# A new instruction order for a fused recurrence and mixture-of-attention kernel, with three small jobs allowed on ScalarE

## The chip, the cores and the metric

The kernel runs on one core of a Trainium2 chip. The metric is the device time of one launch in microseconds (us), lower is better; the median of three runs counts. The core has five engines that run side by side and wait for each other by semaphores: TensorE (PE; its weight loads are listed as PEld), VectorE (DVE), ScalarE (ACT), GpSimd (POOL) and SyncE (SP), which here only issues DMA transfers.

## The reference

The first half is a recurrence over 768 steps for 4 batches and 8 heads with a 48x48 state; its output, rearranged, is the input of the second half, a mixture of four causal attention experts of which each token uses two.

```python
def _attn_ref(r, k, v, w, u):
    for t in range(S):
        kt, vt, rt, wt = (k[:, :, t], v[:, :, t], r[:, :, t], w[:, :, t])
        cur = np.einsum('bhd,bhe->bhde', u[None] * kt, vt)
        y[:, :, t] = np.einsum('bhd,bhde->bhe', rt, state + cur)
        state = wt[:, :, :, None] * state + np.einsum('bhd,bhe->bhde', kt, vt)
    return y

def _moe_ref(x, w_gate, wq, wk, wv, wo):
    logits = x @ w_gate                       # the top K = 2 of E = 4 experts get softmax weights w
    for e in range(E):
        q = x @ wq[e]; k = x @ wk[e]; v = x @ wv[e]
        scores = scale * (q @ k.transpose(0, 2, 1))
        scores = np.where(causal, -1000000000.0, scores)
        a = np.exp(scores - scores.max(-1, keepdims=True))
        a /= a.sum(-1, keepdims=True) + 1e-09
        ye = a @ v @ wo[e]
        for kk in range(K):
            mask = topk[:, :, kk] == e
            out += mask[..., None] * w[:, :, kk:kk + 1] * ye
```

## The kernel before

**Tiling.** The work is cut into eight units (b, g): four batches, and the two halves of 384 steps of each. A unit's recurrence runs over four pairs of heads (p = 0 to 3) in chunks of 64 steps. For each pair SyncE loads the decays, keys and queries (`lt`), the values and keys in natural order (`nat`) and the values (`vy`). VectorE and GpSimd form running products of the decays (`w`, `suf`, lines 518 to 524), scaled keys and queries (`kt` L531, `pre` L533) and the bonus of the current step (`rk`; in the first unit `nat<-lt` L501, in the others `uk` L538, which needs the loaded `u_sb`, and `ur` L542). TensorE transposes the keys (`ktp`), makes the state updates (`ups` L403) and the products inside a chunk (`aps` L587). VectorE masks these (`am` L592) and carries the state from chunk to chunk (`wst` L414, five or six short instructions in a row for each pair). The states are scaled once more (`ys` L424), and TensorE sums up the output (`yps`, L356 and L358). The attention half then runs projections (`pp` L684, `vp` L722), scores (`sp` L789), the row maximum on VectorE (L800), the exponential on ScalarE (L805), transposes (`tp`), weighted sums (`yp` L847), gates and the output projection (`op` L915).

**What sets the order.** Each of these jobs is entered with `plan.add`, with the engines that it may run on. No scheduler decides anything at run time: the table `ORDER` lists every job as a letter for its engine (P, V, A, G, S for TensorE, VectorE, ScalarE, GpSimd, SyncE) and its number. The instructions are issued in exactly this order, so each engine has a fixed queue in which nothing overtakes. Which buffer a tile gets also follows from the table.

Three rules lie on top of the table. A transfer on SyncE waits for the last TensorE instruction that stands ahead of it in the table (`reason="pace"`); a transfer that stands ahead of every product waits for none. GpSimd's two-input jobs wait for the last such job of VectorE ahead of them (`reason="port"`). And a transpose is written as whole products or as two halves, by the mode that TensorE is in when the job comes (`way`).

TensorE works in several tilings: whole array for projections, quarters for the recurrence, halves of rows or columns for scores, half transposes and weighted sums. The table decides how often neighbours in TensorE's queue differ in tiling.

The table also places 14 "warming" products (`warm`, L967), 128x512 products of constants whose results nobody reads. They only keep TensorE busy while the first loads come in.

## Time and profile before

| | |
|---|---|
| time, median of 3 runs | 324.02 us (323.98 to 326.83) |
| profiled execution, its own time | 323.66 us |
| its span, first to last instruction | 321.9 us |
| busy share of the span: PE, PEld | 95%, 77% |
| busy share: DVE, ACT, POOL | 85%, 73%, 46% |
| chain that ended last: PE, DVE, DMA | 75%, 12%, 4% |

The span is 1.76 us shorter than the profiled execution's time; the rest lies around it. The busy time of PE is that of pipelined products whose ends are modelled, so that a PE shown as busy may still have been held up a little. The profile gives busy times by stretch, what ended each idle time of an engine (in square brackets in the rows below), and the chain of work followed back from the last instruction.

### The profile page before, as it was taken

Reading aid. Unit: us, or ns where it says so; the run is one execution under the profiler, and the core shown is the slowest. Engines: PE = TensorE matmul, PEld = TensorE weight load, DVE = VectorE, ACT = ScalarE, POOL = GpSimd, SP = SyncE. Lnnn points to the kernel's source line nnn. Section 1 sums busy time; section 2 is a strip of 40 time slices with the busy share of each in tenths; the row PEclk is TensorE's granted clock in tenths of the full one; section 3 lists DMA queues with packets and bytes.
Section 4 is the critical chain, followed back from the end, with each engine's and each line's share of the span. In section 5 each row is a group of like instructions: output and inputs, shape, how many; then the busy total and the mean of one; then the engine's idle time right before and its main releaser. Section 6 shows DMA issues by size and latency. Waiting matters only on the chain.

```text
span 321.9 us, 13382 instructions
## 1 busy us (share of the span) xinstructions
PE 304.9 (95%) x5334; PEld 247.6 (77%) x5338; DVE 273.0 (85%) x870; ACT 236.4 (73%) x852; POOL 148.3 (46%) x284
## 2 busy tenths in 40 slices
PE   4878999999999899999999999999999999999995
PEld 2755667778876786899887878799888976978684
DVE  6988999999999999999999998977877736575762
ACT  2359799798999898897699776566757664567962
POOL 2225436567375756844667847675121010320420
PEclk9999999999999999999999999999999999999999
DMA  7999574762672789447266472502000001000022
GB/s 230 336 273 227 159 199 142 189 170 60 150 243 75 188 220 227 146 99 195 90 152 178 103 208 72 165 22 88 2 27 0 27 26 52 19 32 24 2 75 74
DMA packets 17758, 39.98 MB, mean 124 GB/s; under 512 B 2592, under 2 KB 10528, under 8 KB 17696
## 3 DMA queue, kind: packets, MB, share of 16 engines
q1 hardware_dynamic: 17696, 39.13, 43.0%
q8 instruction: 42, 0.69, 1.0%
q14 instruction: 20, 0.16, 0.2%
HBM read 34.40 MB, written 4.72 MB: 122 GB/s over the span
## 4 chain that ended last, share of the span: by engine, by line
PE 75%; DVE 12%; DMA 4%; issue 3%; ACT 2%; POOL 2%; SPq 1%; DVEq 0%; ACTq 0%; POOLq 0%
PE pp L684 12%; PE sp L789 11%; PE yp L847 11%; PE op L915 8%; PE vp L722 7%; PE tp L232 5%; PE aps L587 4%; PE ups L403 3%; PE tp L228 2%; PE yps L356 2%; PE yps L358 2%; DMA nat<-in_nat_dram 2%; PE pp L677 2%; DMA lt<-in_wkr_dram 2%; PE ktp L232 2%
## 5 line engine op out<-in xcount | busy, mean ns | idle before, releaser
L805 ACT ACTIVATE a<-a,mx 128x128 f32<-128x128 f32 (+5 forms) x96 | 64.2, 671 | 8.8 <-DVE mx L800 8.6
L800 DVE CUSTOM_DVE_ANT_0 a<-sp,causal 128x128 f32<-128x128 f32 (+5 forms) x96 | 56.6, 614 | 11.0 <-PE sp L789 9.0
L236 ACT COPY ATa<-tp 128x512 f32<-128x512 f32 (+3 forms) x75 | 36.3, 499 | 9.6 <-PE tp L232 8.0
L847 PE MATMUL yp<-ATa,v_sb 128*64 128x384 f32 (+2 forms) x240 | 35.8, 430 | 0.0
L414 DVE SCALAR_TENSOR_TENSOR wst<-wst,suf,ups 112x48 f32<-112x48 f32 x160 | 33.3, 253 | 1.8 <-ACT wst L236 1.3
L684 PE MATMUL pp<-xh,wh_qk 128*128 128x384 f32 x84 | 31.8, 379 | 0.9 <-issue 0.9
L559 ACT ACTIVATE xn<-nat,rk 128x48 f32<-128x48 f32 x126 | 30.7, 329 | 1.0 <-DVE rk L552 1.0
L789 PE MATMUL sp<-K,Q 64*128 64x384 f32 (+4 forms) x160 | 31.1, 420 | 0.4
L684 PE MATMUL pp<-xh,wl_qk 128*128 128x384 f32 x84 | 28.4, 338 | 0.0
L684 PE MATMUL pp<-xl,wh_qk 128*128 128x384 f32 x84 | 28.2, 336 | 0.0
L232 PEld LDWEIGHTS tp<-ident,a 64*128 64x128 f32 x520 | 21.4, 138 | 6.1 <-issue 1.9
L358 PE MATMUL yps<-ys,pre 64*64 64x48 f32 (+1 forms) x704 | 24.7, 220 | 1.1 <-issue 0.6
L232 PE MATMUL tp<-ident,a 64*128 64x64 f32 x520 | 25.3, 226 | 0.4 <-DVE lg L728 0.4
L904 POOL TENSOR_TENSOR yl<-yr,yh 128x384 fp32r<-128x384 f32 x12 | 12.0, 1007 | 29.2 <-ACT yh L903 22.6
L356 PE MATMUL yps<-vy,am 64*64 64x48 f32 x768 | 25.2, 219 | 0.0
L847 PEld LDWEIGHTS yp<-ATa,v_sb 128*64 128x64 f32 x240 | 15.3, 136 | 12.8 <-issue 9.5
L424 POOL TENSOR_TENSOR ys<-wst,suf 112x240 f32<-112x240 f32 (+1 forms) x29 | 23.2, 809 | 3.3 <-DVE wst L414 2.4
L358 PEld LDWEIGHTS yps<-ys,pre 64*64 64x64 f32 (+1 forms) x704 | 21.8, 133 | 3.2 <-POOL ys L424 1.4
L356 PEld LDWEIGHTS yps<-vy,am 64*64 64x64 f32 x768 | 22.6, 134 | 0.1
L550 ACT ACTIVATE nat<-nat 128x48 f32<-128x48 f32 x96 | 22.0, 243 | 0.0
L789 PEld LDWEIGHTS sp<-K,Q 64*128 64x128 f32 x160 | 15.3, 186 | 8.1 <-issue 3.7
L592 DVE TENSOR_TENSOR am<-aps,dec_mask 64x384 f32<-64x384 f32 (+1 forms) x35 | 19.1, 552 | 1.4 <-ACT am L598 0.7
(161 smaller groups left out, 914.3 us busy)
## 6 DMA issues: line engine op xcount, KB each, us to landing
lt<-in_wkr_dram SPq DMA_DIRECT2D x56, 218.6 KB, 3.9
nat<-in_nat_dram SPq DMA_DIRECT2D x28, 432.0 KB, 4.2
vy<-in_vY_dram SPq DMA_DIRECT2D x32, 144.0 KB, 3.5
out_dram<-ob SPq DMA_DIRECT2D x24, 192.0 KB, 1.9
lt<-in_wkr_dram SPq DMA_DIRECT2D x3, 583.0 KB, 5.6
w_qk<-in_wqk_dram SPq DMA_DIRECT2D x1, 768.0 KB, 7.3
nat<-in_nat_dram SPq DMA_DIRECT2D x4, 144.0 KB, 6.7
w_vg<-in_wvg_dram SPq DMA_DIRECT2D x1, 390.0 KB, 7.1
```

Source lines behind the costliest of these rows:

```text
L232: nc.tensor.transpose(o()[:, h * 512 + i * 64:h * 512 + i * 64 + 64], src[r], ident[r, r])
L236: nc.scalar.copy(o, i)
L356: nc.tensor.matmul(to, am()[k, c, :], vy()[k, c, :], start=zero and x == 0, stop=not first and i == 2 and x == len(group) - 1)
L358: nc.tensor.matmul(to, pre()[r, c, 0:C], ys()[r, c, :], start=i == x == 0, stop=False)
L414: nc.vector.scalar_tensor_tensor(new, ws[0:112, c0 + c - 1, :], sfv()[0:112, c, 0:1], upk()[0:112, o], op0=ALU.mult, op1=ALU.add)
L559: nc.scalar.mul(xn()[:, i, (2 * p + h) * D:(2 * p + h + 1) * D], v()[:, i, h, :], rk()[:, i, h:h + 1])
L684: nc.tensor.matmul(pp()[:, 0:384], w[:, qk, k, cs], x()[:, k, :], start=(k == j == 0), stop=(k == j == 2))
L789: nc.tensor.matmul(spv(x)[:, h, :], q_()[p, t], flat(k_())[p, o], start=j == 0, stop=j == len(terms) - 1)
L800: nc.vector.tensor_tensor_reduce(out=a()[:, 0:n].rearrange("p (a n) -> p a n", a=np_), in0=spv(x), in1=causal[:, S - n:S].rearrange("p (a ...
L805: plan.add("exp", {"ACT": t_exp(n)}, lambda e, x=x, y=y, mx=mx, a=a: nc.scalar.activation(a()[:, 0:n], a()[:, 0:n], AF.Exp, bias=mx(), sca ...
L847: nc.tensor.matmul(yp()[e * 64:e * 64 + 64, lo:hi], v_sb[ep]()[:, j, e * 64:e * 64 + 64], at, start=(j == 0), stop=(j == nj - 1))
L915: nc.tensor.matmul(op()[:, 0:DM], y()[:, t], w[:, ep, :], start=(j + ep == 0), stop=(j == 2 and ep == 1))
```

## The change

Three kinds of job get ScalarE as a further choice: scaling the states (`ys`, there as one multiplication for each chunk), the eviction of the gate logits (`lg`, 128x4), and the eviction of the transposed gate weights (`gT`). And the table `ORDER` is replaced as a whole; it still holds the same work and 14 warming products.

```diff
                 def scaled(e, ys=ys, ws=ws, sfv=sfv):
                     o = slice(1 - g, NH)
+                    if e == "ACT":
+                        for c in range(1 - g, NH):
+                            nc.scalar.mul(ys()[0:112, c, :], ws[0:112, c0 + c - 1, :], sfv()[0:112, c, 0:1])
+                        return
...
-                plan.add("ys", {"DVE": t_dve((NH - 1 + g) * D), "POOL": 680 if g == 0 else 645}, scaled, [suf] + [kw + (c0 - g + c,) for c in range(NH - 1 + g)], [ys])
+                plan.add("ys", {"DVE": t_dve((NH - 1 + g) * D), "POOL": 680 if g == 0 else 645, "ACT": 227 * (NH - 1 + g)}, scaled, [suf] + [kw + (c0 - g + c,) for c in range(NH - 1 + g)], [ys])
...
-            plan.add("lg", {"DVE": 70}, lambda e: nc.vector.tensor_copy(lg()[:, i, :], vp()[:, 256:260]), [vp], [(lg, i)])
+            plan.add("lg", {"DVE": 70, "ACT": 100}, lambda e: copy(e, lg()[:, i, :], vp()[:, 256:260]), [vp], [(lg, i)])
...
-            plan.add("gT", {"DVE": 131}, lambda e: nc.vector.tensor_copy(gT(), gp()[0:GROWS, 0:128]), [gp], [gT])
+            plan.add("gT", {"DVE": 131, "ACT": 168}, lambda e: copy(e, gT(), gp()[0:GROWS, 0:128]), [gp], [gT])
...
 ORDER = """
-S110 S111 V1 V2 V117 P13 P21 V118 S3 S137 V114 S136 V119 S170 V122 P33 S195 V121 S113 V120 V123 V142 V139 V124
+S110 V1 V2 V117 S111 V118 V119 S3 S136 S112 S113 S195 S170 P26 P23 P10 V120 V114 V121 S137 V122 V123 V142 V139
...
```

Counted over the whole program, by the tables: `lg` stands 18 times of 24 on ScalarE, `gT` 5 times of 9, `ys` 5 times of 32 (27 multiplications). Of the jobs that had a choice already, many have another engine now. VectorE gives up 4 `uk` and 4 `ur` (GpSimd has them), 2 `pre`, 3 of the value evictions, 2 half-height masks, 1 `kts`, 1 `ys` and 11 short evictions of transposes (128 or 256 columns). It takes on 4 `kt`, 5 evictions of queries and keys, 5 longer evictions of transposes (384 or 512 columns), 2 `ob`, 2 `yl`, 2 `rk`, 2 `rw` (L529) and one each of `w`, `xn` (L561), `wst` copy and full-height mask. That is 51 instructions off VectorE and 26 on. GpSimd's jobs are 6 fewer. On TensorE the places where neighbours differ in tiling are 171 instead of 174; one transpose job is written in halves instead of whole.

The first place is SyncE's queue in the first 20 us. Names: `lt0` to `lt3` are the four buffers of a pair's streams (the second load of `lt0` and `lt1` is for the second unit), `nat000` is unit (0, 0), pair 0, `nat010` unit (0, 1), pair 0. Before, rows 9 to 18 of the queue:

```order
L245 DMA nat000_129<-in_nat_dram 128x288
L245 DMA vy002_150<-in_vY_dram 128x288
L442 DMA lt0_66<-in_wkr_dram 48x1166 x2
L245 DMA vy001_160<-in_vY_dram 128x288
L245 DMA w_qk_169<-in_wqk_dram 128x1536
L442 DMA lt1_67<-in_wkr_dram 48x1166 x2
L245 DMA w_vg_228<-in_wvg_dram 128x780
L245 DMA nat002_167<-in_nat_dram 128x288
L245 DMA nat010_268<-in_nat_dram 128x864
L962 DMA u_sb_90<-in_uN_dram 128x384
```

Of the change, rows 3 to 13 of the queue:

```order
L965 DMA u_t_91<-in_uT_dram 128x8
L245 DMA lt1_67<-in_wkr0_dram 128x1166
L245 DMA nat000_125<-in_nat_dram 128x288
L245 DMA vy000_127<-in_vY_dram 128x288
L245 DMA lt2_68<-in_wkr0_dram 128x1166
L245 DMA lt3_69<-in_wkr0_dram 128x1166
L245 DMA nat001_140<-in_nat_dram 128x288
L446 DMA lt0_66<-in_wkr_dram 48x1166 x2
L966 DMA u_sb_90<-in_uN_dram 128x384
L245 DMA vy001_201<-in_vY_dram 128x288
L245 DMA w_qk_219<-in_wqk_dram 128x1536
```

`nat000` moved from row 9 to row 5, `lt1` one row forward (it stood behind `nat001` in row 4), and `u_sb` from row 18 to row 11, ahead of `w_qk`; `w_vg` went back from row 15 to row 24. Farther on, `lt2` and `lt3` are loaded for the second unit in both; the load that VectorE takes first of the two is now the first one issued.

The second place is VectorE's queue at the second and third pair of the first unit. Names: `w2001` is the decay product of unit (0, 0), pair 1, and `nat001` its bonus. Before, rows 17 to 28:

```order
L518 TENSOR_TENSOR w2001_144<-lt1_67 128x199
L501 TENSOR_TENSOR nat001_127<-lt1_67 128x2x192
L533 TENSOR_TENSOR pre000_147<-lt0_66,w2000_118 128x2x192
L520 SCALAR_TENSOR_TENSOR suf001_152<-w2001_144,one_suf_72 128x198
L527 TENSOR_TENSOR lt1_67<-lt1_67 128x192
L522 RECIPROCAL inv_pre_75<-suf001_152 128x6
L518 TENSOR_TENSOR w2002_158<-lt2_68 128x199
L529 TENSOR_TENSOR lt1_67<-lt1_67 128x192
L531 TENSOR_TENSOR kt001_163<-lt1_67,suf001_152 128x2x192
L520 SCALAR_TENSOR_TENSOR suf002_165<-w2002_158,one_suf_72 128x198
L501 TENSOR_TENSOR nat002_167<-lt2_68 128x2x192
L524 SCALAR_TENSOR_TENSOR w2001_144<-w2001_144,inv_pre_75 128x198
```

Of the change, rows 17 to 28:

```order
L522 TENSOR_TENSOR w2001_145<-lt1_67 128x199
L505 TENSOR_TENSOR nat001_140<-lt1_67 128x2x192
L524 SCALAR_TENSOR_TENSOR suf001_148<-w2001_145,one_suf_72 128x198
L537 TENSOR_TENSOR pre000_150<-lt0_66,w2000_117 128x2x192
L526 RECIPROCAL inv_pre_75<-suf001_148 128x6
L533 TENSOR_TENSOR lt1_67<-lt1_67 128x192
L528 SCALAR_TENSOR_TENSOR w2001_145<-w2001_145,inv_pre_75 128x198
L531 TENSOR_TENSOR lt1_67<-lt1_67 128x192
L522 TENSOR_TENSOR w2003_157<-lt2_68 128x199
L505 TENSOR_TENSOR nat003_159<-lt2_68 128x2x192
L535 TENSOR_TENSOR kt001_184<-lt1_67,suf001_148 128x2x192
L537 TENSOR_TENSOR pre001_238<-lt1_67,w2001_145 128x2x192
```

Pair 3 now comes ahead of pair 2 (its streams are in `lt2`), and the same number of rows stands ahead of the first job on `lt1`.

The third place is TensorE's queue at the start. Before, rows 1 to 12:

```order
L967 LDWEIGHTS causal
L967 MATMUL warm_120<-causal 128x512
L967 LDWEIGHTS causal
L967 MATMUL warm_122<-causal 128x512
L967 LDWEIGHTS causal
L967 MATMUL warm_135<-causal 128x512
L509 MATMUL rk_180<-u_t,nat_129 64x1 x12
L232 MATMUL ktp_197<-ident,kt_142 128x64 x6
L509 MATMUL rk_206<-u_t,nat_127 64x1 x12
L967 LDWEIGHTS causal
L967 MATMUL warm_222<-causal 128x512
L228 MATMUL ktp_224<-ident,kt_163 128x128 x3
```

Of the change, rows 11 to 20 (five warming products stand ahead of these rows):

```order
L971 LDWEIGHTS causal
L971 MATMUL warm_165<-causal 128x512
L971 LDWEIGHTS causal
L971 MATMUL warm_167<-causal 128x512
L971 LDWEIGHTS causal
L971 MATMUL warm_169<-causal 128x512
L513 MATMUL rk_171<-u_t,nat_125 64x1 x12
L232 MATMUL ktp_186<-ident,kt_143 128x64 x6
L513 MATMUL rk_203<-u_t,nat_140 64x1 x12
L403 MATMUL ups_221<-nat_125,kts_196 64x48
```

Eight warming products now stand ahead of the first real one instead of three, and the last of the 14 stands right behind the first `aps`; before, five stood behind the first `yps`, and one came far later. The first `ups`, which needs `nat000`, comes ahead of the second `ktp` instead of behind it.

## Rows read from the trace of the kernel before

**Rows 1.** The page: the span, then busy us, share and instructions by engine.
```profile
span 321.9 us, 13382 instructions
...
PE 304.9 (95%) x5334; PEld 247.6 (77%) x5338; DVE 273.0 (85%) x870; ACT 236.4 (73%) x852; POOL 148.3 (46%) x284
```
**Rows 2.** By stretch: length, busy us of each engine, granted clock, DMA share, GB/s.
```profile
16.00:60.00 44.00, 38.81 (x943) 28.15 (x942) 41.02 (x123) 36.16 (x166) 20.77 (x33) 1.00 0.73 197
60.00:190.00 130.00, 127.93 (x2462) 105.78 (x2461) 125.83 (x401) 112.48 (x433) 83.39 (x143) 1.00 0.59 157
190.00:310.00 120.00, 119.73 (x1709) 98.74 (x1703) 88.54 (x290) 79.62 (x231) 40.28 (x96) 1.00 0.13 43
...
16.00:40.00 24.00, 19.92 (x521) 14.14 (x519) 21.21 (x64) 18.30 (x78) 9.64 (x16) 1.00 0.82 219
```
**Rows 3.** The page: the chain that ended last, shares by engine.
```profile
PE 75%; DVE 12%; DMA 4%; issue 3%; ACT 2%; POOL 2%; SPq 1%; DVEq 0%; ACTq 0%; POOLq 0%
```
**Rows 4.** Timeline of VectorE, 0 to 42 us: start, us, instruction, [idle before, releaser].
```profile
7.35 0.37 DVE L518 TENSOR_TENSOR w<-lt 128x199 f32<-128x199 f32 x1 [0.47 <-DMA lt<-in_wkr_dram]
...
16.25 1.02 DVE L592 TENSOR_TENSOR am<-aps,dec_mask 128x384 f32<-128x384 f32 x2 [0.21 <-PE aps L587]
...
22.83 0.46 DVE L538 TENSOR_TENSOR nat<-nat,u_sb 128x288 f32<-128x288 f32 x1 [0.94 <-DMA u_sb<-in_uN_dram]
...
28.61 0.37 DVE L518 TENSOR_TENSOR w<-lt 128x199 f32<-128x199 f32 x1 [0.75 <-DMA lt<-in_wkr_dram]
```
**Rows 5.** Timeline of SyncE's queue, 0 to 45 us: the issues behind those waits.
```profile
2.85 0.43 SPq L245 DMA_DIRECT2D nat<-in_nat_dram  x1
3.33 1.38 SPq L245 DMA_DIRECT2D lt<-in_wkr_dram  x3
...
16.25 0.33 SPq L962 DMA_DIRECT2D u_sb<-in_uN_dram  x1
...
21.04 2.59 SPq L442 DMA_DIRECT2D lt<-in_wkr_dram  x4
```
**Rows 6.** Waits of SyncE's queue, 0 to 60 us: us in total, times, longest.
```profile
SPq L962 <- PE aps L587: 1.6, 1, 1.6
```
**Rows 7.** Groups by form: busy us, mean ns, idle before.
```profile
L414 DVE SCALAR_TENSOR_TENSOR wst<-wst,suf,ups 112x48 f32<-112x48 f32 x160 | 33.3, 253 | 1.8 <-ACT wst L236 1.3 <-PE ups L403 0.3
...
L538 DVE TENSOR_TENSOR nat<-nat,u_sb 128x288 f32<-128x288 f32 x20 | 10.2, 508 | 0.9 <-DMA u_sb<-in_uN_dram 0.9
...
L531 DVE TENSOR_TENSOR kt<-lt,suf 128x384 f32<-128x384 f32 x13 | 7.4, 582 | 0.0
...
L728 DVE COPY lg<-vp 128x4 f32<-128x4 f32 x24 | 3.7, 153 | 1.9 <-ACT v_sb L236 1.4 <-PE vp L722 0.4
...
L882 DVE COPY gT<-gp 128x128 bf16<-128x128 bf16 x9 | 1.9, 213 | 0.7 <-PE gp L881 0.7
...
L236 ACT COPY wst<-ups 112x48 f32<-112x48 f32 x13 | 2.4, 203 | 4.8 <-DVE wst L414 2.9 <-PE ups L403 1.9
```
**Rows 8.** Timeline, 14 us: runs of short instructions on VectorE and ScalarE.
```profile
14.09 1.47 ACT L559 ACTIVATE xn<-vy,rk 128x48 f32<-128x48 f32 x6
14.14 1.49 DVE L414 SCALAR_TENSOR_TENSOR wst<-wst,suf,ups 112x48 f32<-112x48 f32 x8
```
**Rows 9.** Timeline of TensorE's weight loads around 218 us.
```profile
218.26 0.19 PEld L722 LDWEIGHTS vp<-wl_vg,xh 128*128 128x128 f32 x1
218.38 0.19 PEld L722 LDWEIGHTS vp<-wh_vg,xl 128*128 128x128 f32 x1
218.71 0.79 PEld L587 LDWEIGHTS aps<-pre,kt 64*64 64x64 f32 x48
```
**Rows 10.** Groups by form, PEld: first 0 to 16 us, then 16 to 60 us.
```profile
L587 PEld LDWEIGHTS aps<-pre,kt 64*64 64x64 f32 x48 | 2.7, 205 | 0.0
...
L587 PEld LDWEIGHTS aps<-pre,kt 64*64 64x64 f32 x194 | 4.1, 134 | 0.6 <-issue 0.5
```
**Rows 11.** The chain in order of time, around 29 us: start, us, what.
```profile
29.15 0.76 DVE am L592 x2
```

170 lines of the change are left out of this document (85 added, 85 removed).

## The prediction, made before the changed kernel was run

> **What bounds the kernel now.** I read the page first, then the busy times by stretch, then the waits of the engines that stand idle in them, and the timeline of the first 42 us. The page shows PE busy 304.9 of 321.9 us and DVE 273.0 [rows 1]; the chain that ended last is 75% PE and 12% DVE [rows 3]. The stretches say where. From 60 to 190 us both engines are full: PE 127.93 and DVE 125.83 of 130 us. From 190 to 310 us PE alone is: 119.73 of 120 us, DVE 88.54 [rows 2]. From 16 to 60 us PE is idle for 5.19 us of 44 and DVE for 2.98, and at the very start PE has little to do. So PE can win at most 2.07 us between 60 and 190 us and 0.27 us between 190 and 310 us by standing less idle, and has more to win only ahead of 60 us. There DVE sets the pace: it feeds every state, key and mask that PE's first products need, and it stops for a transfer three times, 0.47, 0.94 and 0.75 us, and once for a product, 0.21 us [rows 4].
>
> **The change, part by part.** The table is replaced as a whole, so I price what differs in sum and look at the places where an engine waits.
>
> *Loads of the first 30 us.* The wait at 7.35 us is for `lt1`. Before, its issue stands behind that of `nat001`, at 2.85 us, and is the first of the three from 3.33 us [rows 5]. The change drops `nat001` from the place ahead of it, so `lt1` can issue 0.48 us earlier; the wait was 0.47 us. The wait at 22.83 us is for `u_sb`. It was issued at 16.25 us, and the queue had stood 1.6 us for `aps` ahead of it [rows 5, 6]; by the pace rule a transfer waits for the product ahead of it in the table. The change puts it right behind the second load of `lt0`, which frees when VectorE's first `pre` is done; even if half of the 6.58 us from issue at 16.25 to its use at 22.83 us is queueing behind others, an issue some 6 us earlier is more than the 0.94 us that were lost. The wait at 28.61 us is for a second load of `lt2` or `lt3`, issued in the run that starts at 21.04 us [rows 5]; the load that VectorE takes first is now issued first, and one pair of issues is about half of the 2.59 us of that run, so 1.3 us against 0.75. All three gone are 2.16 us. What could eat it: the transfers share the same engines, with a DMA busy share of 0.82 between 16 and 40 us [rows 2], so what goes forward pushes `w_vg`, `nat` and `vy` back. `w_vg` went back nine rows; its first reader is a projection after the first unit's recurrence, and I take it as covered; with the cover gone it would cost a wait like the three, below 1 us. Bounds 0 and -2.98 (all of DVE's idle time from 16 to 60 us). I take **-2.2**, the rows' own waits, since each of the three transfers moves by more than it was late.
>
> *VectorE's work.* 51 instructions leave it and 26 come. Each taken by the mean of its group in the view of [rows 7], which shows the largest, the leaving ones sum to 15.9 us (18 `lg` at 0.153, 5 `gT` at 0.213, 8 `uk` and `ur` at 0.508, 20 others at 0.40 on average) and the coming ones to 13.8 us (4 `kt` at 0.582, 22 others at 0.52 on average). But neighbours overlap: a `wst` has a mean of 253 ns [rows 7], and eight of them in a row take 1.49 us, 186 ns each [rows 8], so some 0.07 us of each instruction costs nothing. 25 fewer instructions give back 1.75 of the 2.1 us. I take **-0.4**, with bounds 0 (half of it falls after 190 us, where DVE is idle for 31 us) and -2.1.
>
> *TensorE's tilings.* Neighbouring `vp` loads of one tiling start 0.12 us apart; from the last `vp` to the first `aps`, another tiling, it is 0.33 us [rows 9]: a change of tiling costs 0.21 us. Three fewer are **-0.6**. PE's queue is full where these lie, so I count all of it; bounds 0 and -0.6. The one transpose job in halves is under 0.1 us either way.
>
> *ScalarE's new jobs.* Six multiplications of this shape take 1.47 us, 0.245 each [rows 8]; 27 for `ys` are 6.6 us. A 112x48 copy has a mean of 203 ns [rows 7]; 18 `lg`, no longer than that, are at most 3.7 us, and 5 `gT` by the 213 ns of VectorE's [rows 7] 1.1 us. Other jobs leave ScalarE again for about 2 us. Its idle time is 17.5 us between 60 and 190 us and 40 us between 190 and 310 us [rows 2], which hides the 9.4 us; four of the five `ys` stood at 186 us or later before. The cover fails where such a job stands ahead of an eviction that PE waits for: behind a `ys` that is up to 1.47 us, behind an `lg` 0.2. Queued behind them are the evictions of transposes, and behind these `yp`. Bounds 0 and +4.4 (three `ys` in the way). I take **+0.3**.
>
> *GpSimd* loses 6 jobs at 46% busy: nothing.
>
> *Warming products.* Eight stand at the start instead of three, where PE has nothing else to do; the same 14 remain. Rows: `aps` loads take 205 ns in the first 16 us and 134 ns after [rows 10], though the granted clock reads 1.00 everywhere [rows 2]. So the first 16 us run as at the lower of the clock's levels. More warming at the start could lift it earlier; that would shorten `aps`, for which DVE waited 0.21 us: bounds 0 and -0.2, I take 0. [...]
>
> Sum: -2.2 - 0.4 - 0.6 + 0.3 = -2.9. Against the profiled execution's own 323.66 us that is 320.8; that execution lies 0.36 us below the median of 324.02, so the median should come at **321.1 us**, 0.9% less. It reaches the end because PE and DVE are both full behind 60 us: what starts 2 us earlier there stays 2 us earlier.
>
> **The rivals.**
>
> *More than that* (chance 0.18): the new order also closes the idle time between two full engines, PE's 2.07 us from 60 to 190 us, and DVE's saving counts in full, 1.7 us more. 321.1 - 2.1 - 1.7 = 317.3 us. For it: DVE and PE wait for each other in turn there. Against it: PE is busy for 98.4% already, and another order brings waits of its own.
>
> *No change* (0.26): the load waits only move. The transfers are as many, the DMA share of 0.82 stays, and a wait for `nat`, `vy` or `w_vg` takes the place of the three. 321.1 + 2.2 = 323.3 us; if ScalarE then costs 1 us more, 324.3.
>
> *Slower by TensorE's clock* (0.09): all warming products now stand ahead of about 17 us; before, five came behind the first `yps`. If PE is too thinly busy after that and falls back to the lower level, its work from 16 to 40 us, 19.92 us [rows 2], takes 205/134 times as long [rows 10], 10.5 us more, of which PE's idle 4.08 us there hide a part: +6.4, so 327.5 us. It decides if the lower level lasts for the whole stretch up to the projections; for half of it, +3, and the result is 324. For it: the slow rows of the first 16 us. Against it: PE is busy for 83% of the stretch, and before, with 5.19 us of gaps between 16 and 60 us, the loads kept their 134 ns in the mean [rows 2, 10].
>
> *An engine's queue in a wrong order* (0.05): a job with a late input ahead of one that PE needs, several times; the size is open, 325 to 330 us.
>
> **How the numbers follow.** The forecast, 319.4 to 322.6 us, has 0.42. About 1% (3.2 us) is what this measurement can tell from no change: faster means below 320.8, slower above 327.3 us. Of the forecast's 0.42 I put 0.2 below 320.8; with the first rival that is 0.38 faster. Slower are 0.06 of the clock rival and 0.04 of the last, 0.10. The other 0.52 are within 1%. The range leaves out one in ten on either side: 317.5 to 325.5 us; the forecast's own is 319.4 to 322.6.
>
> **What would show it.** In the changed kernel's profile: VectorE's waits for `lt` and `u_sb` of the first 30 us are gone, and DVE is idle for 1 us or less between 16 and 60 us instead of 2.98. The masks of the first unit's last two pairs, at 29.15 us before [rows 11], start around 26 to 27 us. DVE's busy time is 272 to 273 us, ScalarE's 244 to 247, PE's idle time from 60 to 190 us about 2 us as before. `aps` loads after 16 us stay at 134 ns; if they read 200, the clock has fallen. The prediction is wrong if new waits for a transfer stand in the first 60 us, if PE's idle time between 60 and 190 us is above 4 us with ScalarE as the releaser, or if DVE's gain of the start is lost again before 60 us.

## The result, and the profile after

The changed kernel takes 327.21 us in the median of 20 runs, the kernel before 324.60 in 20 runs beside it. The ratios given here and below leave out runs more than 1.5% above the fastest of their kernel (four of these 20, none of the kernel before); the ratio is then 1.0065, 95% interval 1.0044 to 1.0086: about 2.1 us slower, against 2.6 us between the medians of all runs. The forecast of 321.1 us was wrong in sign, and the time lies outside its range of 317.5 to 325.5 us; it is still within the 1% that I called no change.

The profiled execution of the changed kernel took 326.04 us, its span is 324.3 us; before it was 321.9 [rows 1]. First the page: the span, busy us with share and instructions, the granted clock and the DMA share in 40 slices, and the shares of the chain that ended last.

```profile
span 324.3 us, 13403 instructions
...
PE 305.9 (94%) x5338; PEld 248.4 (77%) x5338; DVE 274.3 (85%) x845; ACT 242.6 (75%) x893; POOL 144.8 (45%) x278
...
PEclk9597799999999999999999999999999999999999
DMA  7999847547726575475636553441100000020022
...
PE 69%; DVE 19%; ACT 4%; issue 4%; POOL 2%; DMA 2%; SPq 0%; DVEq 0%; POOLq 0%; ACTq 0%
```

VectorE has 25 instructions fewer and GpSimd 6, as counted from the tables, and busy times hardly moved. What moved is the chain: PE's share fell from 75% to 69%, and DVE's rose from 12% to 19% [rows 3]. The second, fourth and fifth slices of PEclk fall below 9, where the profile of before read 1.00 in every stretch [rows 2]. Then the stretches (length, busy us of each engine, granted clock, DMA share, GB/s).

```profile
16.00:40.00 24.00, 19.22 (x506) 15.24 (x505) 20.49 (x65) 15.96 (x70) 7.94 (x11) 0.86 0.96 237
16.00:60.00 44.00, 38.08 (x913) 28.86 (x913) 39.30 (x119) 34.45 (x159) 19.55 (x28) 0.92 0.80 207
60.00:190.00 130.00, 124.98 (x2411) 104.43 (x2408) 123.47 (x384) 111.58 (x426) 83.52 (x144) 1.00 0.55 148
190.00:310.00 120.00, 119.83 (x1761) 98.23 (x1760) 92.76 (x288) 85.34 (x277) 37.08 (x89) 1.00 0.17 52
```

Against [rows 2]: from 16 to 40 us the DMA share rose from 0.82 to 0.96 and the granted clock fell from 1.00 to 0.86; from 16 to 60 us VectorE's idle time grew from 2.98 to 4.70 us; from 60 to 190 us TensorE's idle time grew from 2.07 to 5.02 us. Next the timeline of VectorE in the head, its waits from 20 to 40 us (start, us, instruction, idle before and its releaser).

```profile
21.88 0.36 DVE L531 TENSOR_TENSOR lt<-lt 128x192 f32<-128x192 f32 x1 [1.94 <-DMA lt<-in_wkr_dram]
...
29.09 1.02 DVE L596 TENSOR_TENSOR am<-aps,dec_mask 128x384 f32<-128x384 f32 x2 [0.67 <-PE aps L591]
...
39.94 1.02 DVE L542 TENSOR_TENSOR nat<-nat,u_sb 128x288 f32<-128x288 f32 x1 [0.90 <-DMA nat<-in_nat_dram]
```

The three waits of [rows 4] that my first term counted, 0.47, 0.94 and 0.75 us, are gone. In their place stand 1.94 us for another `lt`, 0.67 for `aps` and 0.90 for `nat`. The masks at 29.15 us before [rows 11] are at 29.09 now: nothing was won by then. SyncE's issues in the timeline show why `lt` is late.

```profile
10.97 0.38 SPq L245 DMA_DIRECT2D w_qk<-in_wqk_dram  x1
13.89 0.79 SPq L446 DMA_DIRECT2D lt<-in_wkr_dram  x2
...
27.23 0.42 SPq L245 DMA_DIRECT2D w_vg<-in_wvg_dram  x1
```

The pair of second loads of the second pair's log-decays goes out at 13.89 us, behind the 768 KB of `w_qk`, which took 9.1 us to land. It stood behind `w_qk` before too, went out at 12.69 us, and VectorE did not wait for it; `w_qk` then took 7.3 us. `w_vg`, 390 KB, was issued at 13.6 us before and joins the loads of 27 to 34 us now. TensorE's own timeline shows a standstill that the kernel before did not have there.

```profile
31.45 0.80 PE L403 MATMUL ups<-nat,kts 64*64 64x48 f32 x39
32.18 0.40 PE L232 MATMUL xp<-ident,xn 64*128 64x64 f32 x6
35.18 0.59 PE L232 MATMUL xp<-ident,xn 64*128 64x64 f32 x6 [2.60 <-issue]
35.70 1.56 PE L591 MATMUL aps<-pre,kt 64*64 64x64 f32 x48
```

"issue" means that the engine waited for nothing that the profile shows. Such standstills of 0.5 us or more, called standstills from here on, sum to 4.73 us between 16 and 45 us (1.54, 0.59 and 2.60); before it was one, 1.16 us.

### The profile page after: what moved, and what is told of

It is laid out like the page before. It is cut to its first block, busy times and chain, and to the rows that moved or that the text cites. A ratio compares the mean times of both kernels' runs of the same rounds, so it can differ in the third digit from the quotient of the medians.

```text
span 324.3 us, 13403 instructions
## 1 busy us (share of the span) xinstructions
PE 305.9 (94%) x5338; PEld 248.4 (77%) x5338; DVE 274.3 (85%) x845; ACT 242.6 (75%) x893; POOL 144.8 (45%) x278
## 3 DMA queue, kind: packets, MB, share of 16 engines
q1 hardware_dynamic: 17696, 39.13, 43.3%
## 4 chain that ended last, share of the span: by engine, by line
PE 69%; DVE 19%; ACT 4%; issue 4%; POOL 2%; DMA 2%; SPq 0%; DVEq 0%; POOLq 0%; ACTq 0%
PE pp L688 10%; PE sp L793 10%; PE yp L851 10%; PE op L919 8%; PE vp L726 6%; PE tp L232 5%; PE aps L591 4%; PE pp L681 3%; DVE a L804 2%; PE ups L403 2%; PE yps L358 2%; PE yps L356 2%; DVE w L528 2%; PE tp L228 2%; DVE wst L414 2%
## 5 line engine op out<-in xcount | busy, mean ns | idle before, releaser
L236 ACT COPY ATa<-tp 128x512 f32<-128x512 f32 (+3 forms) x76 | 35.6, 482 | 10.2 <-PE tp L232 7.9
L563 ACT ACTIVATE xn<-nat,rk 128x48 f32<-128x48 f32 x138 | 33.6, 333 | 0.7 <-DVE rk L556 0.7
L236 ACT COPY kts<-ktp 128x384 f32<-128x384 f32 x32 | 14.2, 482 | 9.6 <-PE ktp L232 7.4
L554 ACT ACTIVATE nat<-nat 128x48 f32<-128x48 f32 x84 | 19.2, 239 | 2.9 <-DVE nat L546 2.7
L537 POOL TENSOR_TENSOR pre<-lt,w 128x384 f32<-128x384 f32 x17 | 15.9, 938 | 12.0 <-DVE w L528 4.3
L428 POOL TENSOR_TENSOR ys<-wst,suf 112x288 f32<-112x288 f32 (+1 forms) x25 | 20.4, 826 | 1.1 <-DVE wst L414 1.0
```

The source lines that it names most:

```text
L236: nc.scalar.copy(o, i)
L563: nc.scalar.mul(xn()[:, i, (2 * p + h) * D:(2 * p + h + 1) * D], v()[:, i, h, :], rk()[:, i, h:h + 1])
```

## Where the loss lies: two halves exchanged

Apart from three that load less (k1, k2 and m1 below), every kernel of this study is the kernel before or the changed kernel with its table `ORDER` edited, so a run can take the head of one and the rest of the other.

**The old head, the new rest** (`h1_head_before`).

```diff
 ORDER of the changed kernel:
+the first 298 entries of the kernel before (to about 50 us)
+then the entries of the changed kernel that are left, in its order
```

> The table of before up to about 50 us of the program, then the remaining jobs in the changed table's order. If the loss lies in the first 50 us (clock, loads, ScalarE's order there): 324 to 325 us, as before or better. If it lies behind 50 us (the new order of the full stretch waits more): 326 to 327 us.

**The new head, the old rest** (`h2_head_after`).

```diff
 ORDER of the changed kernel:
+its first 253 entries (to about 46 us)
+then the entries of the kernel before that are left, in its order
```

> The changed table up to about 46 us, then the remaining jobs in the order of before. If the loss lies in the first 46 us: 326 to 327.5 us. If behind: 324 to 325 us. If both share it, this and its mirror image both come at 325.5 to 326.

Measured: the old head with the new rest 1.0016 (0.9989 to 1.0043), the new head with the old rest 1.0102 (1.0057 to 1.0147). The loss is in the head. (The second ratio is above the changed kernel's own 1.0065, by less than the two intervals can tell apart.) One mark makes this readable in any profile: VectorE's first `a<-sp` instruction, the mask of the first attention scores, where the head ends. Timelines of VectorE around it: the kernel before, the changed kernel, old head with new rest, new head with old rest.

```profile
45.65 0.28 DVE L800 CUSTOM_DVE_ANT_0 a<-sp,causal 128x128 f32<-128x128 f32 x1
```

```profile
46.91 0.29 DVE L804 CUSTOM_DVE_ANT_0 a<-sp,causal 128x128 f32<-128x128 f32 x1 [0.34 <-PE sp L793]
```

```profile
46.51 0.28 DVE L804 CUSTOM_DVE_ANT_0 a<-sp,causal 128x128 f32<-128x128 f32 x1
```

```profile
50.64 0.29 DVE L804 CUSTOM_DVE_ANT_0 a<-sp,causal 128x128 f32<-128x128 f32 x1
```

The span less this mark is the rest: 321.9 - 45.65 = 276.25, 324.3 - 46.91 = 277.39, 323.6 - 46.51 = 277.09 and 327.2 - 50.64 = 276.56 us. Over all 20 profiles of this study it hardly varies: the nine with the old rest lie between 276.06 and 277.84, mean 276.75; the eleven with the new rest between 277.05 and 278.41, mean 277.41 (277.44 without g3 and m2 below, the two longest executions). The mark itself lies anywhere from 44.36 to 54.37 us. So what a profiled execution takes is nearly the end of its head plus a constant, and the new rest is **0.7 us longer** (standard error 0.2), not 0.7 us shorter as the terms for VectorE, tilings and ScalarE had it (-0.4 - 0.6 + 0.3). The head's part of the 2.1 us is then about **1.4 us**; between the two profiles it is 1.26. A profile is one execution, and it need not be a typical one: e2's and f1's below are among the fastest of their runs.

The waits of TensorE from 60 to 310 us show where the rest grew: the kernel before, the changed kernel, old head with new rest (us in total, times, longest).

```profile
PE pp L684 <- issue: 0.9, 1, 0.9
PE yps L358 <- issue: 0.6, 1, 0.6
PE ktp L232 <- DVE xl L626: 0.2, 1, 0.2
```

```profile
PE yps L358 <- DVE mx L804: 1.1, 1, 1.1
PE ups L403 <- ACT kts L236: 1.0, 1, 1.0
PE gb L897 <- ACT yr L946: 0.8, 1, 0.8
PE tp L232 <- ACT ATb L236: 0.6, 1, 0.6
```

```profile
PE ups L403 <- ACT kts L236: 0.9, 1, 0.9
PE yps L358 <- DVE mx L804: 0.9, 1, 0.9
PE tp L232 <- ACT ATb L236: 0.7, 1, 0.7
...
PE gb L897 <- ACT yr L946: 0.6, 1, 0.6
```

Before, no wait for ScalarE is listed; now there are 2.4 us, and the same three come again behind the old head (2.2 us). Waits for VectorE's `mx` (1.1 us, and 0.5 us for scores) came with them. In sum TensorE's waits grew by about 3 us and the rest by 0.7 us, so a wait here is not time lost one for one. Do the jobs newly on ScalarE make the evictions late? ScalarE's timeline in the changed kernel has, ahead of `ATb`, `yr` and `kts`, these last waits of its own:

```profile
116.62 0.20 ACT L236 COPY wst<-ups 112x48 f32<-112x48 f32 x1 [0.95 <-DVE wst L414]
...
130.15 0.20 ACT L236 COPY wst<-ups 112x48 f32<-112x48 f32 x1 [1.15 <-DVE wst L414]
...
140.00 0.24 ACT L554 ACTIVATE nat<-nat 128x48 f32<-128x48 f32 x1 [2.73 <-DVE nat L546]
```

Between these rows and the three evictions stands no `lg`, no `gT` and no `ys`. Each time ScalarE had itself waited for VectorE, and the last eviction stands behind twelve short instructions on `nat`, which are no new jobs. So in this profile none of the three is late because a new job stands right ahead of it.

## Loads sent earlier, one or two at a time

My first term said that a load wait that goes is time won. Four runs move loads alone.

**Two loads forward in the kernel before** (`g1_two_loads`).

```diff
 SyncE's entries of the kernel before:
-S110 S111 S3 S137 S136 S170 ... S235 S138 S99 ... S236 S4 S196
+S110 S111 S3 S136 S137 S170 ... S235 S4 S138 S99 ... S236 S196
 (S136 log-decays of pair 1, S4 the bonus rows u_sb)
```

> The kernel before with only two loads sent earlier: the log-decays of the second pair go out ahead of the natives of pair 1 (2.85 instead of 3.3 us), and the bonus rows u_sb right behind the log-decay loads of 8.7 us instead of at 16.25 us. Nothing else moves. These two carry two of the three waits in the first term of my sum (0.47 for lt, 0.94 for u_sb). If a wait that is gone is time gained: 324.8 - 1.4 = 323.4 us, with VectorE's wait for u_sb at 22.8 us gone. If load waits only move, as the run with all the first loads reordered already suggests (it took 326.4): 324.8 +- 0.5, with the same sum of VectorE's waits for loads up to 60 us (2.2 us) at other tiles.

**The first loads in the changed kernel's order, in the kernel before** (`f4_before_loads`).

```diff
 SyncE's entries of the kernel before:
-S110 S111 S3 S137 S136 S170 S195 S113 S112 S172 S235 S138 S99 S250 S104 S171 S236 S4
+S110 S111 S3 S136 S112 S113 S195 S170 S137 S235 S4 S138 S99 S250 S104 S172 S171 S236
```

> The kernel before with SyncE's first loads alone in the changed kernel's order (the second pair of log-decays ahead of the natives of pair 1, the bonus rows u_sb ahead of w_qk), w_qk and w_vg left where the kernel before has them relative to their neighbours, and no job of another engine moved. It measures the first term of my sum by itself. If the three waits of VectorE for loads in the head (0.47 + 0.94 + 0.75) go and nothing takes their place: 322.4 us. If they only move to other loads ('load waits only move', share of the DMA engines near 1 up to 30 us): 324.6 +- 0.6, and VectorE's idle time in 16 to 60 us stays within 0.5 us of 2.98.

**The changed kernel with w_qk behind lt** (`g4_wqk_behind`).

```diff
 SyncE's entries of the changed kernel:
-S4 S138 S99 S250 S171
+S4 S138 S250 S99 S171
 (S99 w_qk, S250 the second log-decays of pair 1)
```

> The changed kernel with the load of w_qk (768 KB) behind the second log-decay load of the second pair instead of ahead of it, one entry of SyncE's order moved: it goes out at about 14.7 us instead of 11.0. The changed kernel's longest wait of VectorE in the head (1.94 us for lt at 21.9 us) should shrink to below 0.7 us. If that wait is time lost: 327.2 - 1.5 = 325.7. If load waits only move: the cast of w_qk on ScalarE (22.2 us in the changed kernel) waits 1 to 2 us for its load instead, the first products of w_qk (24.3 us) start later, and the time is 327.2 +- 0.6.

**The changed kernel with the old order of loads** (`k3_after_sp_before`).

```diff
 SyncE's entries of the changed kernel:
-S110 S111 S3 S136 S112 S113 S195 S170 S137 S235 S4 S138 S99 S250 S171 S196 ... S291 S104
+S110 S111 S3 S137 S136 S170 S195 S113 S112 S172 S235 S138 S4 S99 S250 S104 S171 S196 ...
```

> The changed kernel with the kernel before's order of the loads through the first 50 us or so: the first twelve as there, u_sb behind them, w_vg right behind the second log-decays of the second pair; only SyncE's order differs from the changed kernel. 'Load traffic': the time falls from 327.2 to 325-326. 'Order of jobs' (the other engines' queues of the head make the loss, whichever loads go first): 327 or more, since its own jobs then wait for loads that suit the other order.

Measured, as ratios to the kernel before: two loads 1.0025 (0.9999 to 1.0052); all first loads 1.0050 (1.0021 to 1.0079); w_qk behind lt 1.0061 (1.0028 to 1.0094); old loads in the changed kernel 1.0057 (1.0026 to 1.0089). None is clearly faster than the kernel that it edits. In the first, a gain of 1.4 us would have been a ratio of 0.9957, and the interval leaves it out. VectorE's timeline shows where the waits went.

```profile
7.22 0.37 DVE L518 TENSOR_TENSOR w<-lt 128x199 f32<-128x199 f32 x1 [0.34 <-DMA lt<-in_wkr_dram]
...
23.36 0.46 DVE L538 TENSOR_TENSOR nat<-nat,u_sb 128x288 f32<-128x288 f32 x1 [1.36 <-DMA nat<-in_nat_dram]
...
28.29 0.74 DVE L414 SCALAR_TENSOR_TENSOR wst<-wst,suf,ups 112x48 f32<-112x48 f32 x3 [1.94 <-ACT wst L236]
```

The instruction that waited 0.94 us for `u_sb` [rows 4] now waits 1.36 us for its other operand `nat`, and the wait for `lt1` is 0.34 us where it was 0.47, though its load went out 0.48 us earlier. ScalarE waits 3.89 us for `w_qk` (1.8 before), so that its cast starts 2.2 us later, and the `wst` copy that VectorE awaits at 28.29 us stands behind the later cast of `w_vg` in ScalarE's queue. With `w_qk` put behind, the wait of 1.94 us for `lt` is gone, but VectorE waits 2.64 us up to 25.46 us with nothing shown to wait for, and TensorE stands still twice, 2.08 us up to 24.47 us and 2.80 us up to 37.36 us. In f4 I had also turned the loads of pairs 2 and 3 around, while VectorE still takes pair 2 first: it waited 2.22 us for the one put last. That part is my edit's, so f4 alone would prove little; g1 has no such fault. k3 has it the other way round (the old order loads pair 2 first, VectorE takes pair 3 first), without a wait there, and it keeps `u_sb` ahead of `w_qk`.

## The load of w_vg, and TensorE's standstills

**w_vg back to its early place** (`f1_wvg_early`).

```diff
 SyncE's entries of the changed kernel:
-S99 S250 S171 ... S251 S291 S104 S290
+S99 S250 S104 S171 ... S251 S291 S290
```

> The changed kernel with one entry of SyncE's order moved: the load of w_vg (390 KB, one transfer) goes out where the kernel before sends it, right behind the second load of the second pair of log-decays (about 14.7 us), and not at 27.2 us. Theory 'late instructions': in the changed kernel TensorE stands still for 2.60 us at 32.6 to 35.2 us in the middle of the transposes into xp, with no semaphore to wait for, while the transfers fill their engines (share 1.05 in 30 to 35 us, 0.61 in the kernel before); w_vg is the largest single load of that stretch. Taking it out of the stretch should shrink this standstill to below 1.2 us and bring the time from 327.2 to 325.0-326.2 us. Theory 'order of jobs': the loss comes from the places of the engines' jobs, not from loads; the time stays at 327.2 +- 0.6. A third outcome, that the load now delays the natives behind it (VectorE waits 0.90 us for nat at 39.9 us), would show as a longer wait of VectorE for nat and a time of 327 to 329.

**w_vg later still** (`f2_wvg_late`).

```diff
 SyncE's entries of the changed kernel:
-S291 S104 S290 S367 S237 S352 S305 S252
+S291 S290 S367 S237 S352 S305 S104 S252
```

> The changed kernel with the load of w_vg moved the other way: behind the load of natives that goes out at 33.9 us, so that nothing of it moves between 27 and 34 us. 'Late instructions': the standstill of 2.60 us at 35.2 us shrinks to below 1.2 us; the cast of w_vg on ScalarE (which ran near 42 us) may wait up to 2 us, but its first use by TensorE comes later; time 325.0-326.5. 'Order of jobs': the standstill stays or the time stays at 327.2 +- 0.6.

**The kernel before with w_vg at the new place** (`f3_before_wvg_late`).

```diff
 SyncE's entries of the kernel before:
-S250 S104 S171 ... S251 S290
+S250 S171 ... S251 S104 S290
```

> The kernel before with the one load of w_vg moved from 13.6 us to the changed kernel's place (behind the native load that follows the third and fourth pairs' log-decays, about 27 us). 'Late instructions': with 390 KB more in 27 to 34 us a standstill of TensorE with no semaphore of 1.5 us or more appears between 27 and 37 us, and the time rises from 324.6 to 325.5-326.5. 'Order of jobs': no such standstill, time 324.6 +- 0.6. It can also come out lower: the early loads in 14 to 20 us lose 390 KB of company, so the waits of VectorE for u_sb (0.94) and w (0.75) may go: 323.3-324.

Measured: 1.0094 (1.0061 to 1.0127), 1.0120 (1.0082 to 1.0158) and 1.0143 (1.0111 to 1.0174). The third is my mistake in reading the order: ScalarE's cast of `w_vg` stands early in the old queue, so the queue stopped there for 6.87 us, and behind it the `wst` copies for which VectorE waited 6.9 us in turn. It says nothing about standstills, but shows the price of a load that is late for a fixed queue.

The first did to the standstill what was expected: with `w_vg` early, none stands between 30 and 38 us. It gave no time: VectorE waits 1.81 us for `nat` at 26.59 us instead, which was the third outcome expected, and the median is 328.68 us. (Its profile, with the head ending at 46.62 us, is that of the fastest of its 11 runs, 325.58 us.) The second speaks against `w_vg` as the cause. There `w_vg` goes out at 34.67 us, when TensorE already stands still; the standstill, from 32.64 to 35.95 us, is 3.31 us long instead of below 1.2, and the DMA share from 30 to 35 us is 1.00 with `w_vg` issued only at its end.

Of the eleven profiles with the new head or parts of it, six have a standstill of 2.17 to 4.13 us at `xp`, each with a DMA share of 0.95 or more over the five us in which it begins. Two have a shorter one (1.34 and 0.85 us). Three (f1, k2, k3) have none listed, though the share from 30 to 35 us is 0.99 in k2. In k2 and k3 TensorE does wait at `xp`, 1.87 and 1.36 us, put down to ScalarE's copy into `xh`, which had ended 0.95 and 0.43 us before TensorE went on. The profiles with the old head and all its early loads have a share of 0.62 to 0.70 from 30 to 40 us and no standstill above 0.35 us from 30 to 38 us. In the changed kernel (length, busy us of each engine, granted clock, DMA share, GB/s):

```profile
30.00:35.00 5.00, 2.58 (x142) 2.39 (x133) 5.00 (x16) 3.50 (x12) 0.00 (x0) 1.00 1.05 280
35.00:40.00 5.00, 4.82 (x72) 3.76 (x73) 4.10 (x16) 2.35 (x13) 1.65 (x3) 0.66 0.88 201
```

That TensorE waits for no other engine is plainest in the changed kernel with its warming products moved back (below), where it splits one job of six transposes after the third:

```profile
33.76 0.33 PE L232 MATMUL xp<-ident,xn 64*128 64x64 f32 x3
36.26 0.52 PE L232 MATMUL xp<-ident,xn 64*128 64x64 f32 x9 [2.17 <-issue]
```

The page lists a DMA queue of kind "instruction", 42 packets of 16 KB in the span, 0.9% of the time of the 16 DMA engines; the queue of the loads has 43.3%. The DMA view of 32.2 to 32.4 us of the changed kernel (packets, MB, share of 16 engines) shows one of them start:

```profile
q8 instruction: 1, 0.02, 36.8%
```

By its times in the trace this packet runs from 32.26 to 33.44 us; the standstill ends at 35.18 us, 1.74 us later. This is no single case. The 20 profiles hold 41 standstills of 0.5 us or more behind 14 us, and every one of them ends 1.29 to 1.74 us after the end of such a packet, though the packets of a profile come some 7 us apart on average. That such a packet brings TensorE's own next instructions, and that the standstill ends with them, is my estimate from this timing and the name of the queue; no view shows what a packet holds. Nor is it shown why a packet comes late: no view has the time at which it was asked for, so that the loads hold it up is argued from the DMA shares. The standstills go with the loss: leaving out f3, the seven profiles with 3 us or more of them between 16 and 45 us end their heads at 46.91 to 54.37 us (to 50.76 without g3 and m2), the twelve others (2.3 us or less) at 44.36 to 47.70 us.

## Less to load

**Most of w_qk and w_vg left out, in the kernel before** (`k1_before_few_w`) **and in the changed kernel** (`k2_after_few_w`). The edit is the same in both.

```diff
-        load("wload", f, src, cols, [f])
+        m = cols // 6 if parts == 1 else cols // 12
+        if n != "o":
+            plan.add("wload", {"SP": max(475.0 if cols > 0 else 650.0, abs(cols) * 512 / 360.0)},
+                     lambda e: nc.sync.dma_start(f()[:, 0:m], src[:, 0:m]), w=[f])
...
+            return f()[:, None, 0:m].to_broadcast([128, (o.stop - o.start) // m, m])
...
-            plan.add("ws" + n, {"ACT": t_act(cols // parts) + 40}, lambda e, o=o: nc.scalar.copy(h[:, o], f()[:, o]),
+            plan.add("ws" + n, {"ACT": t_act(cols // parts) + 40}, lambda e, o=o: nc.scalar.copy(shaped(h[:, o]), few(o)),
...
-                        nc.tensor.matmul(pp()[:, 0:384], wf()[:, (qk * 3 + k) * 256:(qk * 3 + k) * 256 + 256][:, cs], xh()[:, k, :],
+                        nc.tensor.matmul(pp()[:, 0:384], wf()[:, 0:128], xh()[:, k, :],
```

> The kernel before with nearly all of two loads left out: of w_qk 64 KB are loaded instead of 768, of w_vg 65 instead of 390, and the casts and products read these columns again and again, so that every engine has the same instructions and the result is another one. It takes 1029 KB out of the transfers of 10 to 25 us. To be read beside the same edit of the changed kernel. Theory 'load traffic' (the head of the changed kernel loses through transfers: late instructions of TensorE, the wait for lt at 21.9 us, and through them the clock): both get faster, the changed kernel by 2 us more than this one, which goes to 323-324. Theory 'order of jobs': both get faster by the same, and the distance of 2.4 us between them stays.

> The changed kernel with the same 1029 KB of w_qk and w_vg left out (the casts and products read the few loaded columns again, so the result is another one; the instructions are the same). 'Load traffic': TensorE's standstills without a semaphore in 16 to 40 us (1.54, 0.59 and 2.60 us in the changed kernel) fall below 1 us in sum, the wait for lt at 21.9 us goes, the mean time at the lower clock level falls from 10.7 to 5 us or less, and the time comes within 0.8 us of the kernel before with the same edit. 'Order of jobs': it stays 2 us or more above that.

Measured: 0.9948 (0.9916 to 0.9979) and 0.9961 (0.9926 to 0.9997). So 1029 KB less are worth 0.5% to the old order and 1.0% to the new one, and the distance between the two falls from 0.65% to 0.13%. The errors of the two ratios together are about 0.5%, so this points to the load traffic of the head as the larger part of the loss and does not settle it; by medians of all runs the distance is 1.6 us against 2.6. Against it stands k3, which came out as the order of jobs had it (327.33 us, forecast 327 or more). In the changed kernel without these loads the wait for `lt` at 21.9 us is gone and the standstill at 35.2 us is no longer listed (the wait of 1.87 us told above is there instead); one of 1.11 us at 23.4 us stays, and the time at the lower clock level did not fall, 8.7 us where 5 or less was expected.

## Warming products and the clock

In the profile of the changed kernel TensorE's granted clock reads 1.00 or 0.50: it is 0.50 from 8 to 14 us, from 25 to 28 and from 36 to 38 us, and a stretch that holds a switch reads between. The 0.50 is called the lower level here. Weight loads for `rk` take 134 ns each from 6 to 7.2 us, where it reads 1.00, and 219 ns from 8.1 to 9.2 us, where it reads 0.50. With 0.50 taken as the lower reading of every run, its mean granted clock gives a time at that level: (1 - clock) x 2 x span. In the compared runs this was 4.0 us for the kernel before (131 runs) and 8.9 us for the changed kernel (16). Within one kernel, over 320 runs of all of them, a run with 1 us more at the lower level is 0.18 us longer (standard error 0.02).

This measure has a hole at the start. Two timelines of TensorE's weight loads, the kernel before and the changed kernel, show the first 24 for `rk`:

```profile
5.35 1.35 PEld L509 LDWEIGHTS rk<-u_t,nat 64*64 64x64 f32 x24 [3.38 <-DVE nat L501]
```

```profile
6.27 0.78 PEld L513 LDWEIGHTS rk<-u_t,nat 64*64 64x64 f32 x24 [2.16 <-DVE nat L505]
```

In the kernel before each of them takes 219 ns, as at 0.50 in the changed kernel, and yet its granted clock reads 1.00 there: by the length of the loads, what lies ahead of the first rise, at about 16 us by the `aps` loads of [rows 10], is not counted. In the changed kernel, behind eight warming products, the clock had risen by then, with 134 ns for each, and fell again; its granted clock reads 0.89 up to 10 us and 0.61 from 10 to 16 us, and this is counted. So of the 13.6 us of its profile some 6.9 lie in a stretch that the kernel before spends at the lower level too, uncounted. The means of kernels with eight products at the start (changed, e2, g3, k2) are too high beside the others by up to this much; five of the nine profiles with eight have such an early rise.

**The changed kernel with its products where the old ones stood** (`e1_warm_back`) **and the kernel before with the new places** (`e2_warm_front`).

```diff
 TensorE's entries of the changed kernel (e1; P5 to P33 here are warming products):
-P26 P23 P10 P8 P15 P5 P20 P16 P115 P126 P140 P128 P33 P21 P151 P18 P153 P161 P30 P13 P28 P174 ...
+P13 P21 P33 P115 P126 P140 P28 P128 P151 P30 P153 P161 P26 P18 P15 P174 ... P229 P16 ... P212 P20 P8 P23 P5 P10
 of the kernel before (e2):
-P13 P21 P33 P115 P126 P140 P28 P151 P30 P128 P153 P161 P26 P18 P15 P199 ...
+P26 P23 P10 P8 P15 P5 P20 P16 P115 P126 P140 P151 P18 P128 P33 P21 P153 P161 P30 P13 P28 P199 ...
```

> The changed kernel with its 14 warming products put back to the places of before (three at the start, two around the second ktp, three behind the first aps, six between the first xp and the first projection); all else as changed. Clock theory (the changed kernel loses time because TensorE falls to its lower level in the first 40 us): granted clock back to 0.99 to 1.00 of the span, median 324.5 to 325.5 us, and less spread than the 324.5 to 331.2 us of the changed kernel. Rival (the order of the real jobs costs the time, the clock is a side effect): 326.5 to 327.5 us whatever the clock.

> The kernel before with its warming products put to the changed kernel's places: eight at the start, the last behind the first aps. Clock theory: the granted clock falls in stretches between 17 and 40 us and the time rises by 1.5 to 3 us against before, to 326 to 327.5 us. Rival: clock may fall, but TensorE is not what the first 40 us wait for; within 0.5 us of before.

**More products: in the kernel before** (`g2_before_more_warm`, and once more as `k4_more_warm_again`), **in the changed kernel** (`g3_after_more_warm`).

```diff
 TensorE's entries of the kernel before (g2, k4): 7 warming products more
-P166 P185 P168 P187 P210 P229 P16 P212 P220
+P166 P6 P7 P185 P168 P9 P187 P11 P210 P12 P14 P229 P16 P212 P17 P220
 of the changed kernel (g3): 8 more
-P174 P166 P168 P210 P185 P229 P199 P187 P212 P1131
+P174 P6 P166 P7 P9 P168 P11 P210 P185 P229 P199 P12 P187 P14 P212 P1131 P17 P19
```

> The kernel before with 7 warming products more, in the stretch 18 to 25 us where TensorE is least busy (two behind the first yps, one behind the second, one behind the third ups, two behind the fourth key transposes, one behind the fourth ups). Over all timed runs so far the kernel before spent on average 4.3 us at the lower clock level, and over all kernels each us there went with 0.2 us of time. Theory 'clock': the mean time at the lower level falls below 2.5 us and the median to 324.0-324.5. Rival 'products stand in the way': each occupies TensorE 0.22-0.38 us ahead of work that is due; the clock gains nothing and the time is 325-326.

> The same kernel as the kernel before with 7 warming products more in 18 to 25 us, timed once more: it had 324.39 against 324.89, ratio 0.9976 with an interval that just reached 1. 'Clock': again 0.3 to 1.0 us faster than the kernel before, mean time at the lower level below 2 us. If the first result was chance: within 0.3 us of it.

> The changed kernel with 8 warming products more between 16 and 25 us (behind the third bonus products, the first and second yps, the fourth bonus products, the third ups and two behind the first product of w_qk). The changed kernel spent on average 10.7 us at the lower clock level. Theory 'clock': this falls to 4-5 us, as in the kernel before, and the time by 0.2 x 6 = 1.2 us, to 326.0. If the clock is the whole of the loss: 324.8. If the products only stand in the way or the level falls all the same: 327.2 or more.

**Old places and 7 more, in the changed kernel with few columns** (`m1_few_w_warm_more`) **and with all loads** (`m2_after_warm_more`).

```diff
 TensorE's entries of the changed kernel: as in e1, and
-P174 P166 P168 ... P199 P187 ... P1131
+P174 P6 P166 P7 P9 P168 P11 ... P199 P12 P187 P14 ... P1131 P17
```

> The changed kernel with both supposed causes taken out: w_qk and w_vg loaded by their first columns alone (1029 KB left out, the result is another one), the 14 warming products at places like those of the kernel before, and 7 more between 16 and 25 us. Two causes were separated: load traffic, which the few columns removed, and the time at the lower clock level, which stayed at 9.2 us in that kernel against 1.8 in the kernel before with the same edit. If the places of the warming products set the clock level: the mean time at the lower level falls from 9.2 to 3 us or less and the median from 325.2 by 0.2 x 6 = 1.3 us to 324.0 or less. If the level falls because of how the other work of the head is ordered: it stays at 7 us or more, and the time at 325.2 or above.

> The same places of the 21 warming products in the changed kernel with all its loads. By the sum of the two causes: lower level from 10.7 to about 4 us, time 327.2 - 1.3 = 325.9, still 1.0 above the kernel before for the load traffic. If the products have no part in the level: 327.2 or more (the changed kernel with its own 14 products alone moved back took 328.3 in 6 runs).

| kernel | us at the lower level, mean | ratio to before |
|---|---|---|
| before | 4.0 | 1 |
| before, new places (e2) | 8.2 | 1.0058 (1.0026 to 1.0091) |
| before, 7 more (g2) | 1.2 | 0.9976 (0.9950 to 1.0001) |
| the same again (k4) | 0.7 | 0.9971 (0.9941 to 1.0002) |
| changed | 8.9 | 1.0065 (1.0044 to 1.0086) |
| changed, old places (e1) | 6.3 | 1.0102 (1.0067 to 1.0137) |
| changed, 8 more (g3) | 9.2 | 1.0042 (1.0009 to 1.0075) |
| changed, old places and 7 more (m2) | 4.0 | 1.0130 (1.0099 to 1.0160) |
| changed, few columns (k2) | 8.7 | 0.9961 (0.9926 to 0.9997) |
| changed, few columns, old places and 7 more (m1) | 1.8 | 1.0072 (1.0046 to 1.0097) |

Two things stand in this table. In the old order the products do what they are for: moving them to the front costs 0.6%, and seven more win about 0.25% in both measurements (24 runs; weighed together 0.9974, interval 0.9954 to 0.9994). In the new order places and number were changed together: the time at the lower level falls from 8.9 to 4.0 us and from 8.7 to 1.8 (in part because the start is then not counted), and the time gets worse each time, by 0.65% and 1.1%. The busy times by stretch suggest a reason. First the kernel before, without and with seven more:

```profile
20.00:25.00 5.00, 2.91 (x118) 2.62 (x119) 4.06 (x12) 2.96 (x13) 0.00 (x0) 1.00 0.87 259
```

```profile
20.00:25.00 5.00, 4.21 (x92) 2.79 (x90) 4.36 (x13) 2.27 (x9) 0.00 (x0) 1.00 0.91 257
```

Then the changed kernel with few columns, with its own 14 products and with the 21:

```profile
20.00:30.00 10.00, 8.84 (x202) 6.70 (x196) 8.13 (x27) 7.67 (x35) 3.74 (x5) 0.83 0.83 231
```

```profile
20.00:30.00 10.00, 9.94 (x196) 6.18 (x189) 6.97 (x25) 7.16 (x32) 3.54 (x5) 1.00 0.82 200
```

In the old order TensorE was busy for only 2.91 us from 20 to 25 us, and the products fill that. In the new order there is less room: 8.84 of 10 us are busy without the products and 9.94 with them, and VectorE's wait for `aps` is 1.77 us with them where it was 1.27. That they delay the work of others is argued from this and not shown, the more so as the profiled execution of m1, 325.23 us, is faster than its median of 326.67 and ends its head at 46.32 us, hardly later than k2's (46.12). What is shown is that less time at the lower level did not make the changed kernel faster.

The fastest kernel of the study that loads everything is thus the kernel before with seven warming products more: 324.39 and 323.94 us in the median, where the kernel before had 324.89 and 325.27.

## Why the prediction was wrong, point by point

**The first term (-2.2 us, loads).** This is the step that failed: I took a wait for a load that goes as time won, "since each of the three transfers moves by more than it was late". The three waits went as forecast, and no time came of it: waits of 1.94, 0.67 and 0.90 us stand in their place, the masks that were to start at 26 to 27 us start at 29.09, and the head ends about 1.4 us later. g1 shows the step by itself: two of the three loads sent earlier give 1.0025 (0.9999 to 1.0052) where 1.4 us were forecast. My bound of 0 was wrong too, since a loss was possible. The few-column runs show that with 1029 KB less in the same stretch time is won, 0.5% and 1.0%. Where the 1.4 us of loss come from is not shown in full; standstills, which no term had, go with them.

**w_vg "covered".** No wait for `w_vg` itself appeared. The share of 30 to 40 us rose from 0.64 to 0.97 and a standstill of 2.60 us came, but f2 shows both with `w_vg` issued only at 34.67 us, so neither can be put down to it. Taking it back (f1) removes the standstill from the profile and moves the wait again.

**VectorE -0.4, tilings -0.6, ScalarE +0.3.** In sum -0.7 forecast, +0.7 measured as the rest behind the head; h1, the new rest behind the old head, has 1.0016 (0.9989 to 1.0043), which leaves out a gain of 0.7 us. VectorE's busy time is 274.3 us (272 to 273 forecast, 273.0 before): with 25 instructions fewer it rose. ScalarE's is 242.6 (244 to 247). TensorE's idle time from 60 to 190 us, which I named as the sign of failure if above 4 us with ScalarE as releaser, is 5.02, with ScalarE among the releasers. But not by the way that the term had priced, a new job ahead of an eviction: the three waits for ScalarE lead back to waits for VectorE. The waits that a whole new order brings were in no term. The three terms were not measured apart.

**Warming products at 0, the clock rival at 0.09.** Its mark was that `aps` loads behind 16 us read 200 instead of 134 ns. In the groups by form from 16 to 40 us of the changed kernel they do:

```profile
L591 PEld LDWEIGHTS aps<-pre,kt 64*64 64x64 f32 x96 | 3.6, 204 | 1.2 <-ACT xn L563 1.1
```

So the clock did fall, as the rival had it. That its time of 327.5 us came within 0.3 us of the median is luck: at 0.18 us per us, 4.9 us more at the lower level are at most 0.9 us, and part of the 4.9 is the start, where the kernel before is at the lower level too; I had put +6.4. The level held for parts of the stretch only: the granted clock reads 0.67 from 25 to 30 us, 0.66 from 35 to 40 us and 0.99 to 1.00 in the rest of 16 to 40 us. In this profile the clock rose behind eight warming products, ahead of the first `rk` loads (134 ns each, where the kernel before, behind three, has 219), and it reads 0.66 from 35 to 40 us, behind the standstill of 2.60 us. That thinly busy stretches bring the clock down, which the rival took as its cause, is not shown by this: from 25 to 28 us it reads 0.50 with TensorE busy for all 3.00 us.

**"No change: the load waits only move" at 0.26, 323.3 us.** This was the nearest true description of the head, and missed the time, since the moved waits for loads are longer (2.84 us in sum against 2.16) and come with standstills.

What stays open: why the new order of the other engines in the head is later by some 1.4 us with either order of loads (k3), how much of that the standstills make, and why the "instruction" packets come when they do.

## What to carry to other kernels

Where transfers fill a stretch (here a DMA share of 0.82 from 16 to 40 us), a wait for a load that disappears is no gain until the profile shows that nothing else waits longer for it; price a reordered load at zero, with bounds on both sides. What won time here was bytes that were not moved. Find one instruction that ends the head of a program and compare its start: in this kernel span less that mark stayed within 1.1 us of its mean over 20 profiles, nine with one rest and eleven with the other, and it told the head's loss from the rest's at once. When an engine stands still with nothing shown to wait for, look at the times of the "instruction" packets in the DMA view. Warming products paid here in a gap that was there in the profile of the very order that they went into (2.91 of 5 us busy); in the order with less of a gap more products came with a longer time.
